# A transformer block on one core: some loads move to GpSimd's queue, weight splitting is spread, statistics go one by one, and three plain steps move ahead of a chunk's last down tiles

## The chip, the core and the metric

The kernel runs on one core of a Trainium2 chip. The metric is the device time in us of one execution. TensorE (PE) does the matrix products, VectorE (DVE), ScalarE (ACT) and GpSimd (POOL) the element work; each engine executes its own instructions in order. SyncE (SP), ScalarE and GpSimd issue DMA transfers; each has a queue of its own.

## What is computed

One block with adaptive layer norm: 32-head attention and a gated feed-forward layer over 2048 rows of width 512, all in 32-bit floats.

```python
B, S, D, F, H = 1, 2048, 512, 1792, 32
mod = (silu(c) @ w_mod)                      # six rows: sa, ca, ga, sb, cb, gb
h = layernorm(x) * (1 + ca) + sa
p = softmax((q @ k^T) * 16 ** -0.5)          # q, k, v from h @ wqkv, head size 16
x = x + ga * ((p @ v) @ wo)
h = layernorm(x) * (1 + cb) + sb
x = x + gb * ((silu(h @ w_gate) * (h @ w_up)) @ w_down)
```

## The kernel before, in words

**Precision.** Every operand of a large product is split into a high part and a low remainder, and three products (high by high, high by low, low by high) are summed. The splitting of `wo`, `w_gate`, `w_up` and `w_down` is done once, on GpSimd, by the generator `split_weights` (L573): it loads a raw piece, copies and subtracts, and stores the split tiles to `wo_dr`, `gu_dr` and `wd_dr` in DRAM. It has 24 pieces of work between its yields: the first loads, two for `wo`, then for each of seven pairs of gate and up tiles one piece for the gate half, one for the up half (in which both finished tiles of 1 MB are stored), and one for the down tile. `after` (L841) advances it by one piece at the end of every fourth step.

**Steps and units.** The order is written out by hand. Attention is cut into 32 units (8 groups of four heads by 4 chunks of 512 query rows) of 16 steps, 512 steps in all. A step has four pairs (`pair_of`, L877): a score product with its exponential on ScalarE (L504, L506), and a product for the row maxima of a unit 19 to 20 steps ahead, reduced on VectorE (L477, L479). Products with V follow (`pvs`). When the maxima of a unit are complete, VectorE combines them, TensorE transposes them, ScalarE copies them out, and SyncE writes them as two extra rows into the query tile (`max_rows`, L489 and L496, `qop<-mr`); the unit's scores read these rows. Keys and queries of the unit after next are loaded at a unit's sixth step (`load_k`, `load_q`, both through L402).

**Closing a unit.** `close_unit` (L823) sends the unit's sums through DRAM (`dn<-o`, `d_dr<-dn`, `rb<-d_dr`) on SyncE's queue, and five steps later GpSimd multiplies (L546) and stores to `o_dr` (L547). After a chunk's last unit, `begin` (L794) makes the chunk's tiles and issues the loads of its x rows (`load_x2`, L639) and of the two output weight tiles (`load_wo`, L644); one step later `load_o` (L659) brings the attention output back on GpSimd's queue, and `split_o` splits it on GpSimd.

**Plain and filled steps.** `plain` runs steps with nothing but attention; VectorE's reductions are then the main work beside TensorE's. `filled` runs two steps and mixes products of an earlier chunk into them: two output pairs (`out_pair`), then the jobs `gate_up` (24 by two products in halves) and `down`. Work on other engines that a finished job causes (the entries of `posts`) is issued by `hook` at the end of such a pair of steps. After an output pair, `add_o` (L726) adds the two row tiles to x and takes their statistics on VectorE. After the second pair, `scaled` (L802) computes the norm's scale (first steps on VectorE, the rest on GpSimd) and normalizes on GpSimd; then 9 plain steps, and 3 in which TensorE transposes the normalized rows (`turned`). A chunk starts at a fixed step (`STARTS`: 147, 275, 403), and the plain steps before the next chunk fill up to it.

**Middle tiles.** A gate tile ends with tanh on ScalarE, two operations on VectorE (L763, L765) and copy and subtract on GpSimd (L766, L767) into a middle tile (`tile_mid`, three buffers). `down` of pair m reads middle tiles 2m and 2m+1. For m below 6 a further gate tile stands between; tile 13 is directly followed by the last down.

**The end.** After step 512, seven jobs of chunk 2 are left (gate tiles 11, 12 and 13, downs of pairs 5 and 6, two halves each), and the whole of chunk 3 follows. The generator `rest` holds the seven jobs, three gate tiles first, then four downs; `take(rest, k)` issues k products between the steps of chunk 3's output projection (L748), of its statistics, `norm_scale` (on VectorE here), `normalize` (on ScalarE here, L687) and `turned`. A down tile has one buffer, so `load_wd` (L654) for pair 6 is issued when pair 5 is done. A spare query tile (`spare`) serves as the fourth middle tile.

Of the kernel before, what the change touches and what calls it, by code (L numbers as in the profile page):

```python
# [19 lines left out]
P = 128  # L20
# [81 lines left out]
def block_kernel(ctx, tc, x, wqkv, wo, w_gate, w_up, w_down, c, w_mod, out):  # L102
# [522 lines left out]
    class Chunk:  # L625
        def __init__(self, ci, x2, oT, hT):
            self.ci, self.x2, self.oT, self.hT = ci, x2, oT, hT
            self.w, self.wd, self.mid, self.mv, self.nt = {}, {}, {}, None, []
            self.places, self.ahead = None, 1
            self.jobs = [(gate_up, (0,)), (gate_up, (1,))]  # L630
            for m in range(NF // FG):
                if m:
                    self.jobs.append((gate_up, (2 * m + 1,)))
                if m + 1 < NF // FG:
                    self.jobs.append((gate_up, (2 * m + 2,)))
                self.jobs += [(down, (m, 0)), (down, (m, 2))]

        def load_x2(self):
            nc.sync.dma_start(self.x2, xd[:, 4 * self.ci:4 * self.ci + 4, :])  # L639

        def load_wo(self, places):
            self.wo = places
            for k, w in enumerate(places):
                nc.sync.dma_start(w.bitcast(F32), wo_dr[k])  # L644

        def load_gu(self, f):
            if f < NF:
# [78 lines left out]
    def add_o(ch, t0, outs):  # L726
# [7 lines left out]
        for e in range(2):  # L734
            t = t0 + e
# [3 lines left out]

    def out_pair(ch, t0, outs, halves):  # L740
        return accumulate(outs, lambda e, a, k: ch.oT[a][:, k, (t0 + e) * P:(t0 + e + 1) * P],
                          lambda b, k: ch.wo[k // 2][:, b, k % 2, :], NK,
                          lambda: posts.append(lambda: add_o(ch, t0, outs)), halves)
# [7 lines left out]
    def gate_up(ch, f, outs, halves):  # L751
# [3 lines left out]
        ch.mid[f] = mid = spare.pop(0) if spare and f == NF - 1 else tile_mid()  # L755
# [36 lines left out]
    side, spare = [], []  # L792

    def begin(ci):  # L794
# [4 lines left out]
        ch.load_x2()  # L799
# [43 lines left out]
    def after(i):  # L843
# [16 lines left out]
        if 0 <= i < UG and i % 4 == 3:  # L860
# [14 lines left out]
    def pair_of():  # L875
# [8 lines left out]
        done += 1  # L884

# [62 lines left out]
    for ci in range(last):  # L948
# [6 lines left out]
        scaled(ch)  # L955
# [4 lines left out]
        for _ in range(len(ch.jobs) - (KEEP if ci == last - 1 else 0)):  # L960
            job, args = ch.jobs.pop(0)
            work = job(ch, *args, outs, True)
# [3 lines left out]
            else:  # L966
                filled(SHORT, work)
    filled(none, iter(()), pairs=4)
# [21 lines left out]
    ch.load_x2()  # L990
    spare.append(pb.tile([P, 2, CW], F32R, name="qop", tag="qop", bufs=3))
    kept = chp.jobs
    rest = whole(chp, [j for j in kept if j[0] is gate_up] + [j for j in kept if j[0] is down])
# [5 lines left out]
    ch.load_o(nc.scalar, (NK - 1,))  # L999
    ch.split_o((NK - 1,), True)  # L1000
    take(rest, 36)
    for t in range(4):
        out_terms(ch, t, banks[t], (NK - 1,))
        if t % 2:
            add_o(ch, t - 1, banks[t - 1:t + 1])
    take(rest, 36)
    ch.norm_scale(nc.vector)
    ch.nt = [v_flat[:, (4 + 2 * k) * D:(6 + 2 * k) * D].rearrange("p (t d) -> p t d", t=2) for k in range(2)]
    for t in range(4):
        ch.normalize(t, True)  # L1010
    ch.places = [tile_gu() for _ in range(2)]
# [5 lines left out]
    take(rest, 24)  # L1017
# [28 lines left out]
```

## Time and profile before

| what | value |
|---|---|
| median of three runs | 1974.08 us (1966.42 to 1975.12) |
| profiled execution | 1970.09 us |
| its span, first to last instruction | 1968.3 us |
| mean granted clock of TensorE | 0.982 |
| busy, share of the span: PE / DVE / ACT / POOL | 96% / 80% / 63% / 21% |
| step 512 ends, last chunk alone from | about 1790.8 us to 1968.3 us |

In the profile, a row such as `PE bank L504 <- DMA qop<-mr` says that TensorE, at line 504 and about to write a bank, waited for the transfer from `mr` to `qop`. Tiles are called by the program's names: `qop` and `kop` are queries and keys, `x` the chunk's rows, `wgu` a gate and up tile (also used for `wo`), `wd` a down tile, `act` the chunk's attention output and later its normalized rows; near the end the last chunk lives in `kop` and `v_flat`. `SPq`, `POOLq` and `ACTq` are DMA issues and waits of those engines.

### The profile page before, as it was taken

What the parts mean: (1) busy time and instruction counts of PE and PEld (TensorE: products, weight loads), DVE (VectorE), ACT (ScalarE), POOL (GpSimd) and SP (SyncE); (2) the same over time, 40 slices, a digit from 0 to 9 for tenths busy, and PEclk for the clock granted to TensorE, in tenths of its full rate; (3) what the DMA queues carried; (4) which work ended last, traced back from release to release, by engine and by line L of the source; (5) the groups of instructions that cost most, each with busy time, mean ns of one, the idle gap of its engine ahead of it and who ended that gap; (6) DMA issues with size and microseconds to landing.
All of it is one profiled execution on the core that took longest, in us unless ns stands there. A gap on an engine that the chain in (4) does not pass through costs nothing.

```text
span 1968.3 us, 40520 instructions
## 1 busy us (share of the span) xinstructions
PE 1892.3 (96%) x16836; PEld 1170.6 (59%) x16836; DVE 1567.9 (80%) x2614; ACT 1240.7 (63%) x2284; POOL 408.2 (21%) x476
## 2 busy tenths in 40 slices
PE   6999999999989999999989999999989999998898
PEld 5766444444455666665455666666454566676687
DVE  5459998999979888887979888888979988822333
ACT  4222887788867666665867666666858866772100
POOL 2000465650013101111113101111112011130321
PEclk9999999999989999999999999999989999999999
DMA  8765676754444434443454334443532345332552
GB/s 283 268 221 130 185 215 204 226 182 85 99 111 100 105 116 120 134 116 85 101 117 97 99 115 131 117 117 95 122 90 53 96 107 147 122 111 103 214 193 107
DMA packets 80756, 267.59 MB, mean 136 GB/s; under 512 B 17364, under 2 KB 22484, under 8 KB 59892
## 3 DMA queue, kind: packets, MB, share of 16 engines
q1 hardware_dynamic: 67660, 212.81, 39.6%
q0 software_dynamic: 12224, 51.39, 7.7%
q8 instruction: 132, 2.16, 0.5%
q10 hardware_dynamic: 688, 0.80, 0.1%
q14 instruction: 52, 0.43, 0.1%
HBM read 201.85 MB, written 62.13 MB: 134 GB/s over the span
## 4 chain that ended last, share of the span: by engine, by line
PE 66%; DVE 24%; DMA 6%; ACT 2%; POOL 1%; issue 1%; SPq 0%; POOLq 0%; ACTq 0%; DVEq 0%
DVE mx L479 23%; PE bank L713 18%; PE bank L519 15%; PE bank L504 13%; PE bank L208 7%; PE bank L721 7%; PE bank L477 6%; DMA qop<-mr 2%; DMA rb<-d_dr 1%; DMA wgu<-gu_dr 1%; DMA qop<-qd 1%; PE bank L161 0%; PE bank L695 0%; DMA wm_ab<-in_w_mod 0%; DMA wd<-wd_dr 0%
## 5 line engine op out<-in xcount | busy, mean ns | idle before, releaser
L479 DVE TENSOR_REDUCE mx<-bank 128x1 f32<-128x512 f32 x2048 | 1302.8, 683 | 161.0 <-PE bank L477 121.3
L504 PE MATMUL bank<-qop,kop 50*128 50x512 f32 x2048 | 780.6, 436 | 32.4 <-DMA qop<-mr 20.6
L477 PE MATMUL bank<-kop,qop 48*128 48x512 f32 x2048 | 794.2, 441 | 6.4 <-DVE mx L479 3.9
L504 PEld LDWEIGHTS bank<-qop,kop 50*128 50x128 f32 x2048 | 360.6, 187 | 339.0 <-issue 82.4
L477 PEld LDWEIGHTS bank<-kop,qop 48*128 48x128 f32 x2048 | 356.5, 187 | 42.1 <-DVE mx L479 18.8
L713 PE MATMUL bank<-act,wgu 64*128 64x512 f32 x1872 | 305.0, 393 | 1.0 <-DVE mx L479 0.5
L713 PEld LDWEIGHTS bank<-act,wgu 64*128 64x128 f32 x1872 | 203.3, 187 | 33.4 <-DVE m L765 2.9
L713 PE MATMUL bank<-wd,mid 64*128 64x512 f32 x912 | 154.4, 399 | 3.0 <-POOL mid L766 2.2
L766 POOL CAST mid<-m 128x512 fp32r<-128x512 f32 x55 | 33.7, 613 | 593.5 <-PE bank L477 266.6
L546 POOL TENSOR_TENSOR on<-o,rb 128x512 f32<-128x512 f32 x31 | 39.7, 1282 | 546.8 <-DMA rb<-d_dr 332.7
L713 PEld LDWEIGHTS bank<-wd,mid 64*128 64x128 f32 x912 | 100.0, 189 | 21.3 <-POOL mid L766 3.0
L759 ACT ACTIVATE th<-bank 128x512 f32<-128x512 f32 x56 | 33.3, 597 | 111.2 <-PE bank L721 76.8
L208 PE MATMUL bank<-hT,wqs 128*128 128x512 f32 x384 | 97.0, 404 | 3.9 <-DVE prt L367 2.4
L763 DVE SCALAR_TENSOR_TENSOR q<-th,bank 128x512 f32<-128x512 f32 x56 | 38.1, 680 | 66.1 <-ACT th L759 66.1
L208 PEld LDWEIGHTS bank<-hT,wqs 128*128 128x128 f32 x384 | 71.5, 191 | 26.2 <-issue 5.9
L778 DVE TENSOR_TENSOR x<-bank,x 128x512 f32<-128x512 f32 x84 | 54.0, 682 | 34.9 <-PE bank L713 20.7
L767 POOL TENSOR_TENSOR mid<-m,mid 128x512 fp32r<-128x512 f32 x55 | 70.9, 1289 | 4.5
L367 DVE TENSOR_TENSOR prt<-bank,prt 128x512 fp32r<-128x512 f32 x32 | 21.9, 688 | 46.7 <-ACT prt L365 46.7
L721 PE MATMUL bank<-wd,mid 128*128 128x512 f32 x204 | 50.3, 398 | 7.8 <-DMA wd<-wd_dr 6.5
L365 ACT CAST prt<-bank 128x512 fp32r<-128x512 f32 x32 | 18.8, 587 | 59.6 <-PE bank L208 46.5
L765 DVE TENSOR_TENSOR m<-bank,q 128x512 f32<-128x512 f32 x56 | 38.7, 691 | 20.5 <-PE bank L721 18.4
L713 PE MATMUL bank<-wgu,act 64*128 64x512 f32 x288 | 48.5, 396 | 0.5 <-issue 0.5
(6274 smaller groups left out, 5112.2 us busy)
## 6 DMA issues: line engine op xcount, KB each, us to landing
wgu<-gu_dr SPq DMA_DIRECT2D x48, 1024.0 KB
kop<-kd SPq DMA_DIRECT2D x62, 768.0 KB
wd<-wd_dr SPq DMA_DIRECT2D x28, 1024.0 KB
gu_dr<-wgu POOLq DMA_DIRECT2D x14, 1024.0 KB, 5.1
qop<-qd SPq DMA_DIRECT2D x64, 192.0 KB
kd<-prt SPq DMA_DIRECT2D x16, 512.0 KB
qd<-prt SPq DMA_DIRECT2D x16, 512.0 KB
kop<-gu_dr SPq DMA_DIRECT2D x8, 1024.0 KB
```

What stands on the lines that cost most here:

```text
L208: nc.tensor.matmul(pt, lhs(a, k), rhs(b, k), start=(n == 0), stop=(n == 3 * nk - 1))
L477: nc.tensor.matmul(pm, qop[u][rows, s, qt * P:(qt + 1) * P], kop[u % 3][rows, s, kc * CW:(kc + 1) * CW], start=True, stop=True)
L479: nc.vector.tensor_reduce(mx[u][:, b, s, qt, kc:kc + 1], pm, op=ALU.max, axis=AX.X)
L504: nc.tensor.matmul(sp, kop[u % 3][rows, h // 2, kt * P:(kt + 1) * P], qop[u][rows, h // 2, :], start=True, stop=True)
L519: nc.tensor.matmul(pv[u][32 * h:32 * h + 32, cols], v_flat[:, e0:e0 + 32], p_[h][:, cols], start=(kt == 0 and half == 0), stop=(kt == 15), ...
L546: mul.tensor_mul(on, o, rb)
L713: nc.tensor.matmul(outs[e], lhs(e, a, k)[rows], rhs(b, k)[rows], start=(ph == 0 and j == 0), stop=(ph == 1 and j == z))
L721: nc.tensor.matmul(outs[e], lhs(e, a, k), rhs(b, k), start=(j == 0), stop=(j == z))
L763: nc.vector.scalar_tensor_tensor(q, th, 1.0, outs[0], op0=ALU.add, op1=ALU.mult)
L765: nc.vector.tensor_mul(m32, outs[1], q)
L767: nc.gpsimd.tensor_sub(mid[:, 1, :], m32, mid[:, 0, :].bitcast(F32))
L778: nc.vector.tensor_add(ch.x2[:, t, :], outs[e], ch.x2[:, t, :])
```

## The change

1. `load_wo` issues on GpSimd's queue instead of SyncE's, and `load_x2` takes the queue: GpSimd's for chunks 0 to 2, ScalarE's for chunk 3, there behind the load of the last part of o instead of ahead of all of it.
2. `split_weights` advances every fifth step (4, 9, ... 124) instead of every fourth (3, 7, ...).
3. Statistics of an output pair, and `scaled`, go into a list `side`, of which each pair takes one entry. At the end of the program `add_o` does them at once, as before.
4. In chunks 0 and 1, three plain steps stand between gate tile 13 and the last two downs. They come off the plain steps ahead of the next chunk.
5. The load of gate tile 12 of chunk 2 is issued in the last steps; a set `loaded` keeps it from being issued twice.
6. At the end the seven jobs keep their own order (tiles 11, 12, two downs, tile 13, two downs), the takes are 48, 24, 24 instead of 36, 36, 24, the loads of chunk 3's gate tiles come after the third, and the spare middle tile is gone.

```diff
-        def load_x2(self):
-            nc.sync.dma_start(self.x2, xd[:, 4 * self.ci:4 * self.ci + 4, :])
+        def load_x2(self, eng):
+            eng.dma_start(self.x2, xd[:, 4 * self.ci:4 * self.ci + 4, :])
...
-                nc.sync.dma_start(w.bitcast(F32), wo_dr[k])
+                nc.gpsimd.dma_start(w.bitcast(F32), wo_dr[k])
...
-            if f < NF:
+            if f < NF and f not in self.loaded:
+                self.loaded.add(f)
...
-        for e in range(2):
-            t = t0 + e
+
+        def sums(t):
             st = pf.tile([P, 6], F32, name="stt", tag="stt", bufs=2)
             nc.vector.bn_stats(st, ch.x2[:, t, :])
             nc.vector.bn_aggr(ch.mv[:, t, :], st)
 
+        for e in range(2):
+            if late:
+                side.append(lambda t=t0 + e: sums(t))
+            else:
+                sums(t0 + e)
...
-        ch.mid[f] = mid = spare.pop(0) if spare and f == NF - 1 else tile_mid()
+        ch.mid[f] = mid = tile_mid()
...
-        ch.load_x2()
+        ch.load_x2(nc.gpsimd)
...
-        if 0 <= i < UG and i % 4 == 3:
+        if 0 <= i < UG and i % 5 == 4:
             next(weights2, None)
...
         done += 1
+        if side:
+            side.pop(0)()
...
-        scaled(ch)
+        side.append(lambda: scaled(ch))
...
             job, args = ch.jobs.pop(0)
+            if args == (NF // FG - 1, 0):
+                plain(WIN)
...
+    chunks[last - 1].load_gu(NF - 2)
     filled(none, iter(()), pairs=4)
...
-    ch.load_x2()
-    spare.append(pb.tile([P, 2, CW], F32R, name="qop", tag="qop", bufs=3))
-    kept = chp.jobs
-    rest = whole(chp, [j for j in kept if j[0] is gate_up] + [j for j in kept if j[0] is down])
+    rest = whole(chp, chp.jobs)
...
     ch.load_o(nc.scalar, (NK - 1,))
+    ch.load_x2(nc.scalar)
     ch.split_o((NK - 1,), True)
-    take(rest, 36)
+    take(rest, 48)
...
-    take(rest, 36)
+    take(rest, 24)
...
+    take(rest, 24)
     ch.places = [tile_gu() for _ in range(2)]
...
     for f in range(ch.ahead):
         ch.load_gu(f)
-    take(rest, 24)
```

SyncE's instructions around the begin of chunk 0, before (`qop<-mr` in the first row belongs to the unit before, in the last row to the unit whose maxima are due at the begin):

```order
L496 DMA qop<-mr 2x8x128 x2
L530 DMA dn<-o 128x1x16
L535 DMA d_dr<-dn 128x16
L540 DMA rb<-d_dr 128x1x512
L402 DMA kop_959<-kd 48x2x2048 x2
L402 DMA qop<-qd 48x2x512 x2
L639 DMA x_5624<-in_A_x 128x4x512
L644 DMA wgu<-wo_dr 128x2048 x2
L496 DMA qop<-mr 2x8x128 x2
```

The same place in the changed kernel:

```order
L496 DMA qop<-mr 2x8x128 x2
L530 DMA dn<-o 128x1x16
L535 DMA d_dr<-dn 128x16
L540 DMA rb<-d_dr 128x1x512
L402 DMA kop_959<-kd 48x2x2048 x2
L402 DMA qop<-qd 48x2x512 x2
L496 DMA qop<-mr 2x8x128 x2
```

The x rows and the two output weight tiles no longer stand between the queries and the maxima. GpSimd's instructions at the same begin, before:

```order
L546 TENSOR_TENSOR on<-o,rb 128x512
L547 DMA o_dr<-on 128x512
L659 DMA act_5626<-o_dr 128x1x512 x4
L664 CAST act_5625<-act_5626 128x512
L665 TENSOR_TENSOR act_5626<-act_5626,act_5625 128x512
```

And in the changed kernel:

```order
L546 TENSOR_TENSOR on<-o,rb 128x512
L547 DMA o_dr<-on 128x512
L639 DMA x_5624<-in_A_x 128x4x512
L644 DMA wgu<-wo_dr 128x2048 x2
L660 DMA act_5626<-o_dr 128x1x512 x4
L665 CAST act_5625<-act_5626 128x512
L666 TENSOR_TENSOR act_5626<-act_5626,act_5625 128x512
```

They now stand between the store of the chunk's last attention output and its loads. ScalarE after the last attention step, before (`kop_86` and `v_flat` hold the last chunk, `th` is the tanh of tiles 11, 12 and 13, L687 normalizes, L700 scales a turned tile):

```order
L547 DMA o_dr<-on 128x512
L659 DMA kop_86<-o_dr 128x1x512
L664 CAST kop_86<-kop_86 128x512
L759 ACTIVATE th<-bank_69 128x512
L759 ACTIVATE th<-bank_67 128x512
L759 ACTIVATE th<-bank_69 128x512
L687 ACTIVATE v_flat<-v_flat,rs_20655,rs 128x512 x4
L700 ACTIVATE h_20793<-bank_63,modc 128x512
```

And in the changed kernel:

```order
L547 DMA o_dr<-on 128x512
L660 DMA kop_86<-o_dr 128x1x512
L639 DMA v_flat<-in_A_x 128x4x512
L665 CAST kop_86<-kop_86 128x512
L766 ACTIVATE th<-bank_69 128x512
L766 ACTIVATE th<-bank_67 128x512
L688 ACTIVATE v_flat<-v_flat,rs_20668,rs 128x512 x4
L766 ACTIVATE th<-bank_69 128x512
L701 ACTIVATE h_20789<-bank_63,modc 128x512
```

The load of x stands behind that of the last part of o, and the tanh of tile 13 stands behind the normalizing instead of ahead of it.

More of the change, by code (lines that the diff above doesn't have):

```diff
@@ L628, in __init__ @@
             self.w, self.wd, self.mid, self.mv, self.nt = {}, {}, {}, None, []
-            self.places, self.ahead = None, 1
+            self.places, self.ahead, self.loaded = None, 1, set()
             self.jobs = [(gate_up, (0,)), (gate_up, (1,))]
@@ L724, in accumulate, with add_o @@
                     yield
-    def add_o(ch, t0, outs):
+    def add_o(ch, t0, outs, late):
         if ch.mv is None:
@@ L742, in out_pair @@
                           lambda b, k: ch.wo[k // 2][:, b, k % 2, :], NK,
-                          lambda: posts.append(lambda: add_o(ch, t0, outs)), halves)
+                          lambda: posts.append(lambda: add_o(ch, t0, outs, True)), halves)
     def out_terms(ch, t, pt, ks):
@@ L791, in block_kernel @@
     chunks = {}
-    side, spare = [], []
+    side = []
     def begin(ci):
@@ L1004, in block_kernel @@
         if t % 2:
-            add_o(ch, t - 1, banks[t - 1:t + 1])
-    take(rest, 36)
+            add_o(ch, t - 1, banks[t - 1:t + 1], False)
+    take(rest, 24)
     ch.norm_scale(nc.vector)
```

## The prediction

> **What bounds the kernel now.** I read the page first, then TensorE's waits, then the places of the longest waits in the chain, in SyncE's issues and in the windows table.
>
> ```profile
> PE 1892.3 (96%) x16836; PEld 1170.6 (59%) x16836; DVE 1567.9 (80%) x2614; ACT 1240.7 (63%) x2284; POOL 408.2 (21%) x476
> DVE  5459998999979888887979888888979988822333
> ```
>
> TensorE is busy 96% of the span, so an edit can only remove what makes it stand still or run at half clock, or shorten the stretches where VectorE (the digits 9, the plain steps) sets the pace. TensorE's waits, in us in total, times and longest:
>
> ```profile
> PE bank L504 <- DMA qop<-mr: 20.6, 4, 6.4
> PE bank L721 <- DMA wd<-wd_dr: 6.5, 1, 6.5
> PE bank L748 <- ACT kop L664: 4.1, 1, 4.1
> PE bank L713 <- POOL mid L766: 2.2, 2, 2.0
> PE bank L477 <- DMA qop<-qd: 1.4, 1, 1.4
> PE bank L713 <- POOL mid L767: 0.8, 2, 0.4
> ```
>
> The change touches every one of them. The biggest is a small transfer: the two row maxima of a unit (8 KB each) that go into the query tile before its scores. SyncE's issues before the first of these waits, and the transfer's pieces in the chain (start, length):
>
> ```profile
> 522.47 0.90 SPq L402 DMA_DIRECT2D kop<-kd  x2
> 523.42 1.44 SPq L402 DMA_DIRECT2D qop<-qd  x2
> 524.90 0.46 SPq L639 DMA_DIRECT2D x<-in_A_x  x1
> 525.59 0.84 SPq L644 DMA_DIRECT2D wgu<-wo_dr  x2
> 545.23 1.34 SPq L496 DMA_DIRECT2D qop<-mr  x2
> ...
> 545.23 9.30 DMA qop<-mr
> 302.56 5.51 DMA qop<-mr
> ```
>
> At a chunk's begin the maxima stand in SyncE's queue behind about 5 MB: keys and queries (2 x 768 and 2 x 192 KB), x (1 MB) and the output weights (2 MB). They land 9.30 us after the first issue. The wait of 6.4 belongs to this place, so they are needed 9.30 - 6.4 = 2.9 us after issue.
>
> What such a wait costs is more than its length. Windows: start:end, width, busy us of PE, PEld, DVE, ACT, POOL, granted clock, DMA share, GB/s. The first is an undisturbed plain stretch, the next three are the chunk begins, the fifth is the wait at 302, the sixth the late queries.
>
> ```profile
> 505.00:525.00 20.00, 20.00 (x204) 9.49 (x202) 20.00 (x35) 17.14 (x34) 0.00 (x0) 1.00 0.09 22
> 545.00:565.00 20.00, 13.61 (x118) 6.08 (x118) 11.50 (x19) 10.19 (x20) 7.41 (x8) 0.74 0.38 97
> 985.00:1005.00 20.00, 14.02 (x127) 6.38 (x130) 12.39 (x21) 10.21 (x21) 7.40 (x8) 0.83 0.45 108
> 1420.00:1440.00 20.00, 14.30 (x121) 6.25 (x117) 12.36 (x22) 10.30 (x21) 7.72 (x9) 0.74 0.52 135
> 305.00:315.00 10.00, 7.40 (x50) 3.27 (x50) 5.45 (x10) 5.11 (x11) 8.59 (x9) 0.68 0.63 216
> 380.00:390.00 10.00, 8.56 (x69) 3.54 (x61) 8.59 (x16) 5.87 (x13) 9.15 (x10) 0.83 0.78 250
> ```
>
> VectorE sets the pace there, so its missing busy time is time lost: 20.00 - 11.50 = 8.5, 20.00 - 12.39 = 7.6, 20.00 - 12.36 = 7.6, together 23.7 us; at 302 it is 4.55, at 380 it is 1.4. The excess over the wait is the clock, granted at 0.68 to 0.83 in these windows.
>
> The Trainium skill ("TensorE: Matmul & The Clock Gate", Part 1) drops the clock only after an idle window of about 3.4 us. The row at 302 (a wait of 5.51 - 2.9 = 2.6 us) disagrees, since the clock fell after it. By the rule a remaining wait of 2.6 us would cost just that instead of 4.55, and the first term below would be about 4 us larger.
>
> **The change part by part.** *x and output weights to GpSimd's queue.* SyncE's maxima now have nothing large ahead but keys and queries, issued 22 us earlier. Yet the 3 MB still move then, out of another queue into the same engines. Is the maxima's time then the ordinary one, at most 2.9, or that of 302? There the other queue was full:
>
> ```profile
> q0 software_dynamic: 428, 2.60, 87.3%
> ```
>
> In 298 to 306 GpSimd's queue alone took 87.3% of the engines, and the maxima took 5.51. GpSimd issues at the first begin:
>
> ```profile
> 531.71 1.82 POOL L659 DMA_DIRECT2D act<-o_dr  x3
> 556.70 1.27 POOL L665 TENSOR_TENSOR act<-act,act 128x512 fp32r<-128x512 f32 x1
> L713 PE MATMUL bank<-wgu,act x96: 385/392/498, 565.3 to 590.6; 64*128 64x512 f32 x96
> ```
>
> x and weights will be issued at 531.7, just ahead of these loads of o. With 3 MB and four times 256 KB, 4 MB, at 250 GB/s (estimated between the 216 and the 325 that 2.60 MB in 8 us make) the queue is full until about 548, so the maxima at 545 meet it. Bounds of the remaining loss per begin: 0 and 4.55; below zero is excluded, since the maxima cannot land before they are needed with profit. I take 3.6, nearer to 302, whose queue was as full. Gain: 23.7 - 3 x 3.6 = 12.9 us, bounds 10.0 and 23.7.
>
> The same FIFO puts the loads of o behind 3 MB. Today the last split of o ends at 556.7 + 1.3 = 558.0, and its first use is at 565.3. All the bytes are the same and the engines were full until about 552 anyway, so o comes at most a few us later, in order of use, while the chunk starts some 5 us earlier: cost 0, hidden by these 7 us; without that cover it would be 2 to 4 us per begin.
>
> *Weight splitting every fifth step.* Work per splitting step is unchanged, its cover is the plain steps. The two-store steps of a pair of tiles stood one step before the maxima at 302 (step 43 and maxima at 44); now they stand at 24, 39, 54, and so on, never within three steps before maxima. This removes 4.55, and perhaps the 1.4 at 380:
>
> ```profile
> 368.33 14.40 DMA qop<-qd
> ```
>
> But loads of keys and queries come at steps 21, 37, 53, 69, 85, 101, 117, and the two-store steps at 24, 39, 54, 69, 84, 99, 114: every load now meets one. Queries took 14.40 there with a wait of 1.4, so 13.0 us are free. I charge three new losses of the 1.4 kind, 4 us. Net gain 4.55 + 1.4 - 4 = 2, bounds -6 and +6.
>
> *Statistics one by one.* After the second output pair VectorE runs two adds, two statistics and the scale's first steps in a row, and TensorE starves. Windows again; the first is ordinary chunk work, the second a chunk's end, the third the statistics.
>
> ```profile
> 900.00:920.00 20.00, 19.64 (x204) 12.87 (x204) 17.11 (x27) 13.02 (x23) 1.29 (x1) 1.00 0.62 145
> 920.00:930.00 10.00, 7.72 (x42) 4.64 (x46) 5.04 (x9) 3.47 (x6) 2.49 (x3) 0.66 0.26 68
> 1035.00:1045.00 10.00, 8.70 (x65) 3.51 (x61) 9.32 (x21) 6.12 (x13) 6.53 (x22) 0.83 0.00 0
> ```
>
> VectorE sets the pace after it, so 10.00 - 9.32 = 0.7 is lost, three times: gain 2, bounds 0 and 4 (TensorE's own gap of 1.3, three times). Norm scaling starts three pairs later, under nine plain steps.
>
> *Three plain steps ahead of the last down tiles.* The last down needs the middle tile of the gate tile right before it. At 920 TensorE waits 2.0 + 0.4 and the clock falls: VectorE does 5.04 where ordinary work does 17.11 / 2 = 8.56, so 3.5 / 8.56 of 10 us are lost, 4.1 us. The other of the two times is the rest of 2.2 + 0.8, that is 0.6 us. The moved steps are taken from the stretch before the next chunk, at one price. Gain 4.7, bounds 0 and 4.7.
>
> *The end.* TensorE's rows after the last attention, then the end of the norm scale on VectorE, the normalizing on ScalarE, and two groups of the page:
>
> ```profile
> 1799.04 8.42 PE L721 MATMUL bank<-act,wgu 128*128 128x512 f32 x36
> 1811.60 5.49 PE L748 MATMUL bank<-kop,kop 128*128 128x512 f32 x12 [4.13 <-ACT kop L664]
> 1825.30 5.66 PE L721 MATMUL bank<-wd,mid 128*128 128x512 f32 x24
> 1837.86 1.62 PE L721 MATMUL bank<-wd,mid 128*128 128x512 f32 x3 [6.46 <-DMA wd<-wd_dr]
> 1846.33 2.47 PE L721 MATMUL bank<-kop,wgu 128*128 128x512 f32 x10
> ...
> 1826.31 0.17 DVE L683 TENSOR_SCALAR rs<-rs 128x4 f32<-128x4 f32 x1
> 1826.51 2.94 ACT L687 ACTIVATE v_flat<-v_flat,rs,rs 128x512 f32<-128x512 f32 x4 [3.12 <-DVE rs L683]
> L778 DVE TENSOR_TENSOR x<-bank,x 128x512 f32<-128x512 f32 x84 | 54.0, 682 | 34.9 <-PE bank L713 20.7
> L767 POOL TENSOR_TENSOR mid<-m,mid 128x512 fp32r<-128x512 f32 x55 | 70.9, 1289 | 4.5
> ```
>
> 48 products at 8.42 / 36 = 0.234 last from 1799.0 to 1810.3, so the wait for the last part of o shrinks from 4.13 to about 1.3 and its 12 products run in 2.8 at full clock: done at 1814.4. The next wd tile is asked for after the earlier downs, one gate tile (5.6 us) before its use: the 6.46 goes. What is late next is the normalizing: VectorE's chain from 1811.6 to 1826.5 gets two adds of 0.682 more, and ScalarE ends at 1826.5 + 1.4 + 2.9 = 1830.8. TensorE reaches the transposes at about 1829.4, because the second down's bank is read behind the statistics. Then the last middle tile, whose tanh stands behind the normalizing on ScalarE and whose copies stand behind those of the first turned tile on GpSimd, takes about 3.4 us (two pairs of copies, each 1.3 and about 0.6). The remaining products and transposes took 1846.33 - 1837.86 = 8.5. So the last chunk starts at 1830.8 + 3.4 + 8.5 = 1842.7, against 1846.3: gain 3.6, and 0.5 from a shorter load chain with x no longer beside it: 4. Bounds: 0 (x, now behind the last o on ScalarE's queue, 2 us late, and half clock) and 8.
>
> Sum: 12.9 + 2 + 2 + 4.7 + 4 = 25.6. The profiled execution took 1970.09 with a span of 1968.3; 1970.1 - 25.6 = 1944.5. It lies 4 under the median of the runs and 4 above the fastest; the four executions average 1.3 above it, so I forecast 1945.
>
> **The rivals.** *The queue was everything* (0.2): maxima from an otherwise empty queue land in 2.9 us. For it: 28 of 32 units show no wait, some with weight traffic. Against it: 302. All 23.7 come back, the splitting gains 6: 23.7 + 6 + 2 + 4.7 + 4 = 40.4, 1930. The Trainium skill ("DMA: Bandwidth & Descriptors", Queues, rings and completion order) says that each DMA engine goes round between its queues packet by packet; that speaks for this one.
>
> *The engines were everything* (0.2): the maxima land as late as before whatever their queue, and 12.9 falls to 0 to 3. For it: 302, and the full engines. The sum is 13 to 16, 1955, and 1964 if the end gives nothing either. The same page (Issuing engines are not separate DMA queues) says that all issuers' transfers interleave on the same 16 engines and only issue time is saved.
>
> *Slower* (0.06): the splitting's new rhythm. If each of the seven loads of keys and queries lands 6 us later than the 13.0 that are free, each costs what a chunk begin costs now, about 8: 56 lost instead of 4, 1944.5 + 52 = 1997. It decides from 5 us per load on, where 25.6 is eaten up. Against it: the looser rhythm moves fewer bytes in any 13 us than now.
>
> **How the numbers follow.** My forecast, 1937 to 1953, has 0.54. Between it and the rivals the cases run from 1928 to 1963, with 1 in 10 left out on either side. About 0.5%, 10 us, is what a measurement can tell from no change: faster means under 1964. The forecast and the first rival are (0.74), and 0.08 of the second, whose rest is within: 0.82 faster, 0.12 within, 0.06 slower.
>
> **What would show it.** Right: the waits for maxima at the three begins fall from about 6 to 1 to 3 us, with windows there at 16 or more of 20; no wait for wd near the end; the middle tile's wait gone in the chunks; the last chunk's first gate tile starts some 26 us earlier. Wrong: waits of 5 us or more for maxima at the begins, waits for keys or queries in the splitting steps, a wait for the output weights or o at a chunk's start, or a TensorE gap over 5 us before the last chunk's transposes.

## The result and the profile after

Four executions of the changed kernel took 1949.57 us in the median (1946.00 to 1950.91), four of the kernel before beside them 1974.17 (1966.42 to 1975.12). The ratio is 0.9881, with a 95% interval of 0.9853 to 0.9909. The profiled execution took 1946.00 with a span of 1944.2, against 1970.09 and 1968.3: 24.1 us of span are gone, and the mean granted clock is 0.992 against 0.982.

From the page: the engines' busy times hardly differ from before, so what went is standing still and half clock.

```profile
PE 1884.0 (97%) x16836; PEld 1166.5 (60%) x16836; DVE 1568.0 (81%) x2614; ACT 1241.2 (64%) x2284; POOL 415.6 (21%) x487
```

**Where the time went.** Each unit's maxima are sent off by one pair of issues on SyncE (L496), in both kernels at the same place of the program. They serve as milestones. Issue times, and the lengths of the stretches between them:

| stretch, by units | before | after | gain |
|---|---|---|---|
| start to 1 | to 182.72 | to 181.78 | 0.94 |
| 1 to 9 (weight splitting) | to 504.38: 321.66 | to 502.03: 320.25 | 1.41 |
| 9 to 10 | to 545.23: 40.85 | to 542.87: 40.84 | 0.01 |
| 10 to 11 (begin of chunk 0) | to 604.33: 59.10 | to 597.03: 54.16 | 4.94 |
| 11 to 16 | to 885.03: 280.70 | to 877.68: 280.65 | 0.05 |
| 16 to 18 (last downs of chunk 0) | to 986.99: 101.96 | to 974.30: 96.62 | 5.34 |
| 18 to 19 (begin of chunk 1) | to 1045.21: 58.22 | to 1029.96: 55.66 | 2.56 |
| 19 to 24 | to 1325.85: 280.64 | to 1310.59: 280.63 | 0.01 |
| 24 to 26 (last downs of chunk 1) | to 1423.36: 97.51 | to 1407.17: 96.58 | 0.93 |
| 26 to 28 (begin of chunk 2) | to 1524.33: 100.97 | to 1503.44: 96.27 | 4.70 |
| 28 to 32 | to 1733.31: 208.98 | to 1712.48: 209.04 | -0.06 |
| 32 to the end | to 1968.3: 234.99 | to 1944.2: 231.72 | 3.27 |

The gain falls where the change put its edits: 12.2 at the three begins (queue and statistics together), 6.3 at the two chunk ends, 3.3 at the end. The 1.4 in the splitting is no measured gain: six profiled executions that have the same code there take 318.5 to 323.7 us, and the kernel before took 318.10 when it was profiled again. The first row's 0.9 lies ahead of every edit; executions differ there by up to about 3 us, which is why stretches and not only spans are compared below.

TensorE's waits of the changed kernel (us in total, times, longest):

```profile
PE bank L504 <- DMA qop<-mr: 11.2, 4, 3.9
PE bank L722 <- DVE q L770: 5.0, 1, 5.0
PE bank L722 <- POOL mid L773: 3.5, 2, 2.7
...
PE bank L477 <- DMA kop<-kd: 0.8, 1, 0.8
PE bank L477 <- DMA qop<-qd: 0.8, 1, 0.8
```

The wait for wd (6.5) and that for the last part of o (4.1) are gone; the maxima are still waited for, four times. SyncE's issues at chunk 0's begin, and the transfers in the chain:

```profile
520.09 0.90 SPq L402 DMA_DIRECT2D kop<-kd  x2
521.04 1.30 SPq L402 DMA_DIRECT2D qop<-qd  x2
542.87 1.34 SPq L496 DMA_DIRECT2D qop<-mr  x2
...
303.38 5.20 DMA qop<-mr
443.13 16.26 DMA qop<-qd
542.87 6.25 DMA qop<-mr
974.30 6.83 DMA qop<-mr
1407.17 5.54 DMA qop<-mr
```

SyncE has issued nothing else for 20 us, yet these 16 KB take 6.25 us, where 2.9 would do. At the three begins they take 6.25, 6.83 and 5.54 (before 9.30, 8.88, 8.51) and are waited for 3.3, 3.9 and 2.6. GpSimd's rows at that place say what is in the way (start, length, in brackets the idle time before and what ended it):

```profile
529.35 0.77 POOL L639 DMA_DIRECT2D x<-in_A_x  x1
530.10 1.08 POOL L644 DMA_DIRECT2D wgu<-wo_dr  x2
...
547.83 0.61 POOL L665 CAST act<-act 128x512 fp32r<-128x512 f32 x1 [9.87 <-DMA act<-o_dr]
554.24 1.28 POOL L666 TENSOR_TENSOR act<-act,act 128x512 fp32r<-128x512 f32 x1
```

x and the output weights go out at 529.35 and 530.10, and o, in the same queue behind them, is there only by 547.83, so the queue is at work when the maxima are issued at 542.87. Windows of the changed kernel: the three begins, the end of chunk 0, the statistics of chunk 1 (start:end, width, busy us of PE, PEld, DVE, ACT, POOL, granted clock, DMA share, GB/s):

```profile
541.00:561.00 20.00, 16.51 (x150) 8.20 (x152) 14.75 (x24) 12.05 (x24) 7.37 (x8) 0.83 0.32 80
972.00:992.00 20.00, 15.72 (x138) 6.72 (x136) 13.78 (x23) 11.39 (x23) 7.37 (x8) 0.83 0.37 88
1405.00:1425.00 20.00, 17.07 (x162) 9.07 (x162) 16.05 (x27) 13.37 (x26) 7.39 (x8) 0.91 0.28 70
...
915.00:935.00 20.00, 19.30 (x193) 11.74 (x191) 17.89 (x31) 13.42 (x25) 2.19 (x4) 1.00 0.16 56
...
1019.00:1030.00 11.00, 10.35 (x101) 4.55 (x92) 10.54 (x25) 6.80 (x14) 3.46 (x18) 1.00 0.10 41
```

At the begins VectorE misses 5.2, 6.2 and 3.9 of 20 us, 15.4 together, where it missed 23.7 before. At the chunk's end and in the statistics the clock is full again (before 0.66 and 0.83).

The end, TensorE's rows:

```profile
1778.31 11.17 PE L722 MATMUL bank<-act,wgu 128*128 128x512 f32 x48
1789.31 2.93 PE L755 MATMUL bank<-kop,kop 128*128 128x512 f32 x12
...
1799.96 4.60 PE L722 MATMUL bank<-wd,mid 128*128 128x512 f32 x12 [4.95 <-DVE q L770]
...
1813.94 2.14 PE L722 MATMUL bank<-wd,mid 128*128 128x512 f32 x3 [2.74 <-POOL mid L773]
1822.03 2.46 PE L722 MATMUL bank<-kop,wgu 128*128 128x512 f32 x10
```

The 12 products with the last part of o follow the 48 without a wait, and no wait for wd is left. A wait of 4.95 stands in their place, for VectorE's part of gate tile 12, which is queued there behind the adds and statistics; and these are late because x is:

```profile
1782.76 0.86 ACTq L639 DMA_DIRECT2D v_flat<-in_A_x  x1
1793.64 1.29 DVE L734 TENSOR_TENSOR v_flat<-bank,v_flat 128x512 f32<-128x512 f32 x2 [4.83 <-PE bank L722]
DMA to landing us min/median/max: 10.1/10.2/10.5
```

The last row is that of all loads of x. The last chunk's is issued at 1782.76 and so lands at about 1793.0, 0.6 before the adds; the products for the first add ended about 2 us before that. (The row of the adds names a TensorE bank; releasers are inferred. In three of the experiments below, which have the same code here, VectorE's idle time ahead of these adds, 2.0 to 2.9 us, is put down to `DMA v_flat<-in_A_x`.) From the first product of the output projection to the last chunk's first gate tile it is 1822.03 - 1770.01 = 52.0 us, against 1846.33 - 1790.75 = 55.6 before (the starts are TensorE's first L755 and L748 rows).

### The profile page after: what moved, and what is told of

Its sections match the earlier page's. It is cut to its first block, busy times and chain, and to the rows that moved or that the text cites. A ratio compares the mean times of both kernels' runs of the same rounds, so it can differ in the third digit from the quotient of the medians.

```text
span 1944.2 us, 40515 instructions
## 1 busy us (share of the span) xinstructions
PE 1884.0 (97%) x16836; PEld 1166.5 (60%) x16836; DVE 1568.0 (81%) x2614; ACT 1241.2 (64%) x2284; POOL 415.6 (21%) x487
## 4 chain that ended last, share of the span: by engine, by line
PE 69%; DVE 25%; DMA 3%; ACT 2%; POOL 0%; issue 0%; SPq 0%; POOLq 0%; ACTq 0%
DVE mx L479 23%; PE bank L714 18%; PE bank L519 16%; PE bank L504 13%; PE bank L722 7%; PE bank L477 7%; PE bank L208 6%; DMA qop<-mr 1%; DMA qop<-qd 1%; PE bank L755 1%; DVE stt L738 1%; PE bank L696 0%; PE bank L161 0%; DMA wm_ab<-in_w_mod 0%; PE bank L277 0%
## 5 line engine op out<-in xcount | busy, mean ns | idle before, releaser
L722 PE MATMUL bank<-wd,mid 128*128 128x512 f32 x216 | 55.9, 410 | 9.2 <-DVE q L770 5.0
L722 PEld LDWEIGHTS bank<-wd,mid 128*128 128x128 f32 x216 | 41.7, 196 | 20.4 <-DVE q L770 5.4
```

The source lines that it names most:

```text
L722: nc.tensor.matmul(outs[e], lhs(e, a, k), rhs(b, k), start=(j == 0), stop=(j == z))
```

## The experiments

The theory: the maxima's time depends on the order in their queue and also on what other queues move at that moment, so the change shortened the begins without clearing them. The rivals: that only the bytes in flight count (then the queue's change bought nothing), and that the begins were never about the queue. Further ones concern the other parts. "After" is the changed kernel; each experiment changes it by the lines shown. Gains are read between the milestones of the table, in one profiled execution of each kernel; where several kernels have the same code at a place, their range says how much a single difference is worth. Kernels that were run several times beside the kernel before have a ratio to it; the others were run once.

### The queue alone undone

```diff
-                nc.gpsimd.dma_start(w.bitcast(F32), wo_dr[k])
+                nc.sync.dma_start(w.bitcast(F32), wo_dr[k])
...
-        ch.load_x2(nc.gpsimd)
+        ch.load_x2(nc.sync)
```

> The changed kernel with the x rows of chunks 0 to 2 and all output weight tiles back on SyncE's queue; the rest of the change stays. Theory (queue order counts): the waits for the row maxima at the three begins go back from 3.3, 3.9 and 2.6 us to about 6 each, and the span grows by 8 to 10 us (the loss at the begins is 23.7 us in the kernel before and 15.4 us in the changed one), to about 1953. Rival (only the bytes in the 16 engines count, whatever the queue): the waits stay near 3 us and the span within 2 us of 1944.

Measured: 1959.56 us, ratio 0.9938 (0.9920 to 0.9956), span 1950.9. TensorE's wait and the transfers in the chain of this kernel:

```profile
PE bank L504 <- DMA qop<-mr: 17.1, 3, 6.7
```

```profile
542.02 9.60 DMA qop<-mr
977.90 8.32 DMA qop<-mr
1411.83 7.88 DMA qop<-mr
```

The old landing times are back. From unit 10 to 11, 18 to 19 and 26 to 27 it takes 58.67, 56.83 and 56.44 us; after takes 54.16, 55.66 and 52.79. So the queue alone is worth 4.5 + 1.2 + 3.6 = 9.3 us against the changed kernel's profile, and 6.9 to 8.7 against four further executions with the same begins as the changed kernel. The whole time agrees: the interval of the ratio lies above that of the changed kernel (0.9853 to 0.9909), and the profiled execution, 1952.73, was the fastest of ten. The rival that only bytes count has fallen. The begin of chunk 1 gains least: there the clock falls as far with the short wait (0.83 in the window) as with the long one before (0.83).

### The loads of x and weights some 20 us earlier

```diff
-                at(i + 6, lambda: begin(u // NG))
+    for c in range(last):
+        at(16 * NG * (c + 1), lambda c=c: begin(c))
```

Nothing is left out; begin(c) now comes at steps 128, 256 and 384, ahead of the store of the chunk's last attention output.

> The changed kernel with the begin of chunks 0 to 2 (loads of x rows and output weights) at steps 128, 256 and 384, some eight steps earlier, so that these 3 MB have mostly moved before the row maxima are due. Theory (what is left of the waits is the full DMA engines): the waits for the maxima at the begins fall from 3.3, 3.9 and 2.6 us to under 1 and the span falls by 10 to 15 us, to 1929 to 1934. Rival (what is left is the path of this transfer itself, or GpSimd's queue): the waits stay at 3 us, span 1942 to 1946. A second rival: the early loads press on the keys and queries issued then; waits for queries appear, of 1 to 3 us, and half of the gain is lost.

Measured: 1947.24 us, ratio 0.9872 (0.9839 to 0.9904), span 1944.6: no faster than after. At chunks 1 and 2 no maxima are waited for any more, which shows that the 3 MB were what they met. At chunk 0, GpSimd is ahead of its steps and issues x at 501.18; so the bytes met the maxima of the unit before, issued at 505.66, which took 7.06 and were waited for 2.9. Even at chunk 1, where the wait has gone, not all of its time came back. From the wait list of 935 to 990, from VectorE's rows, and a window:

```profile
PE bank L477 <- DVE mx L479: 0.8, 1, 0.8
```

```profile
976.07 0.71 DVE L485 TENSOR_SCALAR nm<-m 128x16 fp32r<-128x16 f32 x1
976.81 0.52 DVE L486 SCALAR_TENSOR_TENSOR nm<-m,nm 128x16 fp32r<-128x16 f32 x1
```

```profile
980.00:985.00 5.00, 5.00 (x37) 1.79 (x29) 2.81 (x5) 1.83 (x4) 2.39 (x3) 0.50 0.01 3
```

A single wait of 0.8 us, and the clock was granted at 0.50 for the next 5 us. The little operations that combine the maxima took 0.71 and 0.52 us while GpSimd was splitting o beside them; in the kernel before, where GpSimd is idle at that point, they take 0.18 and 0.17. The stretch from unit 17 to 19 is 3.4 us shorter than before (after: 0.95), 25 to 27 is 5.35 shorter (after: 3.85), and 9 to 11 only 2.7 (after: 4.95). The cause of the waits is thus shown; that their whole cost comes back with them is not.

### Early begin with chunk 0 on SyncE's queue, and the splitting of o later

```diff
-                at(i + 6, lambda: begin(u // NG))
+    for c, i in enumerate((126, 256, 384)):
+        at(i, lambda c=c: begin(c))
...
-                nc.gpsimd.dma_start(w.bitcast(F32), wo_dr[k])
+                (nc.gpsimd if self.ci else nc.sync).dma_start(w.bitcast(F32), wo_dr[k])
...
-        ch.load_x2(nc.gpsimd)
+        ch.load_x2(nc.gpsimd if ci else nc.sync)
```

Besides, `split_o` is called at step i + 11 instead of i + 9. SyncE issues in time with the steps, so chunk 0's bytes go out right behind one unit's maxima (x at 507.11, the maxima at 505.73 and 547.79).

> The changed kernel with the loads of x rows and output weights early and apart from other work: for chunk 0 on SyncE's queue right behind the maxima of step 124, for chunks 1 and 2 on GpSimd's at steps 256 and 384; and the splitting of o two steps later, behind the two small VectorE steps that make the maxima. Theory (the full engines held the maxima, and beside GpSimd's splitting VectorE's small steps run three times as long and the clock falls): no wait for maxima over 1 us at any begin, clock 1.0 there, and 10 to 14 us less from the maxima before a begin to those after it, three begins together; span 1930 to 1935. Rival (the loss moves on: the later splitting is late for the output products): TensorE waits for the split o at a chunk's start, 1 to 3 us each, and the span stays above 1938.

Measured: 1939.76 us, ratio 0.9865 (0.9835 to 0.9894), span 1936.1. The interval overlaps that of the changed kernel, so the stretches have to tell the two apart. The begins:

```profile
545.00:565.00 20.00, 19.52 (x176) 10.33 (x176) 18.00 (x31) 14.32 (x28) 4.35 (x5) 0.91 0.01 2
972.00:992.00 20.00, 19.20 (x185) 10.46 (x187) 19.41 (x35) 16.29 (x32) 6.36 (x7) 1.00 0.04 14
1400.00:1420.00 20.00, 18.73 (x179) 10.10 (x176) 19.48 (x33) 15.66 (x30) 6.11 (x7) 1.00 0.03 9
```

VectorE is busy 18.00 to 19.48 of 20 us at all three; no maxima are waited for there. Against before, 9 to 11, 17 to 19 and 25 to 27 gain 7.5, 7.2 and 6.7 us, 11.6 more than after does. So the 15.4 us that the changed kernel still loses at its begins were for the most part the loads'. The other half of the edit did nothing: GpSimd splits o when o lands, whatever the step, and at 972.60 and 972.94 the little operations ran beside it as in the run above, and took 0.30 and 0.52. That the clock held here and not there is not explained by the later call. The last experiment below has the same code at that place and gained 4.9 and 7.0 us from 17 to 19 and from 25 to 27, with a clock of 0.91 and 1.00 in these two windows. Of the eight begins of this kind in the three early-begin kernels, the clock fell (to 0.50 to 0.79 in a window of 5 us) after waits for VectorE of 0.7, 0.8, 1.1 and 1.1 us, and held at 1.00 after 0.5, 0.6, 0.9 and 0.9. What decides it is open.

### The three plain steps taken out

```diff
-            if args == (NF // FG - 1, 0):
-                plain(WIN)
```

> The changed kernel without the three plain steps ahead of the last down tiles of chunks 0 and 1. Theory (the last middle tile is late there, since GpSimd stands waiting for the reciprocals): the wait of 2 us and the half clock after it come back in chunk 0, and the span grows by 5 to 6 us (5.3 and 0.9 by the times of the maxima), to about 1950. Rival (the plain steps only shift the phase of the queues): the wait for the middle tile stays under 0.5 us and the span changes by under 2 us.

Measured: 1951.53 us, ratio 0.9900 (0.9868 to 0.9932), span 1949.8; the interval overlaps that of the changed kernel. From 16 to 18 it takes 97.30 us and from 24 to 26 97.56; after takes 96.62 and 96.58. The plain steps are worth 0.7 + 1.0 = 1.7 us here, not the 6.3 of the table. The rest belongs to something else, which the next run was to find.

### The kernel before, once more

Unchanged.

> The kernel before, unchanged, profiled a second time. Theory (the long wait at the end of chunk 0, about 2.4 us with the half clock after it, came from a store on GpSimd that stood 1.73 us before it was issued, which some executions have and some don't): if the gap is again 1.7 us, the wait for the middle tile is 2 us or more; if it is 0.3 us, the wait is under 0.8 and this stretch is 4 to 5 us shorter. Rival (the wait belongs to the kernel): 2 us or more whatever the gap. The waits for the maxima at the begins are again 5.5 to 6.5 us under either.

Measured: 1966.06 us, span 1964.3. GpSimd's store at the end of chunk 0, in the run without plain steps and then here:

```profile
917.56 0.58 POOL L547 DMA_DIRECT2D o_dr<-on  x1 [0.30 <-POOL on L546]
```

```profile
916.64 0.60 POOL L547 DMA_DIRECT2D o_dr<-on  x1 [1.73 <-DVE mx L479]
```

```profile
920.00:930.00 10.00, 9.35 (x80) 6.05 (x78) 7.68 (x12) 5.76 (x10) 1.10 (x2) 0.83 0.17 62
```

The issue of the store comes 1.73 us after the multiplication instead of 0.30. In the kernel before the middle tile's copy is queued right behind it on GpSimd, and TensorE, which needs that tile for the last down, waits 1.7 + 0.4 here (2.0 + 0.4 in the first profile) and then runs at 0.83 of the clock. 16 to 18 takes 100.40 us. With plain steps, the same delay of 1.73 was there in the kernel with the queue undone, and 16 to 18 took 96.61, as after did without the delay. So the three plain steps are worth 0.7 us where the store is issued at once, and 100.40 - 96.61 = 3.8 to 101.96 - 96.61 = 5.3 where it is delayed.

The delay goes with the kernel, not with the execution. In each of the twelve traces of this document exactly one DMA issue of GpSimd stands about 1.7 us behind its data with no wait that accounts for it (the releaser named above is inferred). In five traces it is this store: the kernel before twice, the queue undone, the second early begin and the last experiment, in all of which chunk 0's x and output weights go out on SyncE's queue. In the seven in which they go out on GpSimd's it is an earlier store, at 627 to 633; in the changed kernel:

```profile
626.73 0.65 POOL L547 DMA_DIRECT2D o_dr<-on  x1 [1.69 <-issue]
```

Ahead of the late issue GpSimd has issued 64 transfers in each of the five and 62 in each of the seven. At its earlier place it costs nothing: 11 to 16 takes 280.65 us in the changed kernel, 280.70 before. So the queue's edit, by putting three more transfers into GpSimd's queue, also moves the late issue away from the chunk's end. That is where most of the gain from 16 to 18 came from: without the plain steps it is already 101.96 - 97.30 = 4.7 us of the 5.3. Why one issue is late at all is open.

### Statistics at once

```diff
-            add_o(ch, t0, outs, True)
+            add_o(ch, t0, outs, False)
...
-        side.append(lambda: scaled(ch))
+        scaled(ch)
```

> The changed kernel with the statistics of an output pair and the norm's scale issued at once, as before. Theory (TensorE starves behind the burst and the clock falls): a TensorE gap of about 1 us and a granted clock of 0.8 to 0.9 come back after the second output pair of each chunk, and the stretch from a chunk's begin to the next maxima is 1 to 1.5 us longer, 3 to 4 us in all. Rival (VectorE has the same work either way): under 1 us in all.

Measured: span 1948.0. From the second add to the next maxima's issue it takes 10.50, 11.85 and 11.85 us at the three chunks; after takes 10.44, 10.43 and 10.46, before 11.86, 11.85 and 11.85. The window at chunk 1 of this kernel, beside after's at 1019:

```profile
1020.00:1032.00 12.00, 10.69 (x95) 4.65 (x87) 11.18 (x24) 6.44 (x13) 6.46 (x22) 0.86 0.09 36
```

With all at once the clock falls to 0.86, one by one it stays at 1.00. That is 1.4 us a chunk; at chunk 2 the next unit gives 0.8 of it back (42.70 here, 43.49 after). Against the kernel before, the statistics are worth 3 x 1.4 - 0.8 = 3.4 us. Against this run it is 2.1, since at chunk 0 the burst did no harm here, and against the second profile of the kernel before 2.8, where it did none at chunk 2 (10.46). One by one, all 27 stretches of nine profiles lie between 10.40 and 10.81.

### Splitting every fourth step

```diff
-        if 0 <= i < UG and i % 5 == 4:
+        if 0 <= i < UG and i % 4 == 3:
```

> The changed kernel with the weight splitting advanced every fourth step again. Theory (the two rhythms cost about the same, each losing at other places): from the first maxima to those of unit 9 the time is within 2 us of the changed kernel's 320.3 us, where the kernel before took 321.7. Rival (the spread splitting is a gain of its own): 3 us or more longer.

Measured: span 1946.7. From unit 1 to 9 it takes 319.57 us, after takes 320.25 and before 321.66, all within the 318.5 to 323.7 of equal code. The old rhythm inside the new kernel is no slower: the spread splitting has no gain that these runs can tell from none. Where it loses, it loses as the others do: maxima of 5.15 us at 303.12, queries of 15.27 at 366.52.

### The last chunk's x first

```diff
+    ch.load_x2(nc.sync)
     rest = whole(chp, chp.jobs)
...
-    ch.load_x2(nc.scalar)
```

> The changed kernel with the last chunk's x rows loaded as before, on SyncE's queue ahead of the last load chain; the rest stays. Theory (x arrives late behind the last part of o: issued at 1782.8, needed by about 1790.8, used at 1793.6): the additions of the output projection start 2 to 3 us earlier, TensorE's wait of 5.0 us in the downs shrinks to 2 to 3, and the span falls by 2 to 3 us, to about 1942. Rival (x beside the load chain of o delays that chain by as much): the last part of o is split 1 to 2 us later, and the span stays within 1 us of 1944.

Measured: 1949.90 us, ratio 0.9891 (0.9859 to 0.9923), span 1947.1. The wait for tile 12 falls from 5.0 to 2.2 us, and a new one of 1.5 for the last part of o takes its place. From the output projection to the first gate tile it is 1824.93 - 1773.45 = 51.5, against 52.0, and 50.4 to 52.4 in the seven profiles with the changed kernel's end (in which the wait for tile 12 is 2.8 to 5.0): x ahead of the short chain of loads delays that chain by nearly as much as it saves. Moving a megabyte ahead of another need only chooses which of the two is late.

### The old order of the last jobs

The seven jobs as in the kernel before (three gate tiles, then four downs, takes of 36, 36 and 24, the spare middle tile), with x still behind o on ScalarE's queue.

```diff
-    rest = whole(chp, chp.jobs)
+    spare.append(pb.tile([P, 2, CW], F32R, name="qop", tag="qop", bufs=3))
+    kept = chp.jobs
+    rest = whole(chp, [j for j in kept if j[0] is gate_up] + [j for j in kept if j[0] is down])
...
-    take(rest, 48)
+    take(rest, 36)
```

> The changed kernel with the old order of the seven jobs at the end (three gate tiles first, takes of 36, 36 and 24, the spare middle tile back), but x still behind the last part of o on ScalarE's queue. Theory (the new order removes the wait for the down tile and shortens the one for o, and gives part back at the statistics): from the output projection's first product to the last chunk's first gate tile it takes 55 to 56 us as in the kernel before, against 52.0, and the wait for wd of 6 us is back. Rival (the gain came from x no longer beside the load chain): 52 to 53 us.

Measured: span 1951.4, and 1829.28 - 1774.87 = 54.4 us for the stretch. TensorE's rows:

```profile
1792.65 3.29 PE L755 MATMUL bank<-kop,kop 128*128 128x512 f32 x12 [1.06 <-ACT kop L665]
...
1819.84 1.62 PE L722 MATMUL bank<-wd,mid 128*128 128x512 f32 x3 [4.44 <-DMA wd<-wd_dr]
```

The wait for wd is back with 4.44. So of the 3.6 us that the end gained, 2.4 are the order of the jobs and 1.2 the place of x; against the mean of the seven profiles with the changed kernel's end, 51.3, the order gives 3.1. With the same 36 products ahead of it as in the kernel before, the last part of o is waited for 1.06 us instead of 4.13: with x out of its chain of loads it is there 3.1 us earlier. A wait of 3.39 for tile 12, behind the late x, takes most of that back.

### The early begins, and x of the last chunk four steps before the end

The kernel of early begin with chunk 0 on SyncE's queue, and:

```diff
-    ch.load_x2(nc.scalar)
+    at(n - 4, lambda: chunks[last].load_x2(nc.gpsimd))
...
+    take(rest, 25)
...
-    take(rest, 24)
```

The third take now stands ahead of the normalizing loop, so that tile 13's tanh comes before it on ScalarE.

> The kernel with the early loads at the begins and the later splitting of o, and at the end two more edits: the last chunk's x rows are loaded on GpSimd's queue four steps before the last step, ahead of the load chain, and gate tile 13 is issued ahead of the normalizing, with one product of the last downs, so that its tanh and its middle tile come before those of the turned rows. Theory (x late, then the middle tile late, is what is left at the end): the wait of 5.0 us in the downs falls to 1 to 3, that of 2.7 for the middle tile under 0.5, the stretch from the output projection to the last chunk's first gate tile falls from 52.0 to 46 to 49, span 1930 to 1934. Rival (VectorE's chain sets this stretch): waits move to the transposes, and the stretch stays above 50.

Measured: 1932.60 us (1925.74 to 1937.08), ratio 0.9798 (0.9762 to 0.9834), span 1930.7: the fastest version, 0.8% below the changed kernel by the ratios, whose intervals don't touch. TensorE's rows:

```profile
1783.78 2.93 PE L755 MATMUL bank<-kop,kop 128*128 128x512 f32 x12
...
1791.09 3.04 PE L722 MATMUL bank<-wd,mid 128*128 128x512 f32 x12 [1.60 <-DVE q L770]
...
1808.41 2.46 PE L722 MATMUL bank<-kop,wgu 128*128 128x512 f32 x10
```

The stretch takes 1808.41 - 1764.49 = 43.9 us against 52.0, and the wait for tile 12 falls from 4.95 to 1.60. The wait for tile 13's middle tile falls from 2.74 to 0.40. Here x is early without standing ahead of o, and 8.1 us come back, so the late x and the late tile 13 together were what bounded the changed kernel's end; this run doesn't separate them.

## Why the prediction was right, point by point

**The sum.** 25.6 us were forecast against the profiled execution, 24.1 were found, and nearly all of the gain lies in the forecast stretches. That the sum came so close is in part luck: the maxima fell about 4 us short of their term, the chunk ends gave 1.6 more than theirs for a reason that the prediction didn't have, and 0.9 lies ahead of every edit. Three steps failed: the price of the remaining loss at the begins, the cause of the wait at chunk 0's end, and the place of the next wait at the end. Two numbers don't follow from their working: two pairs of copies of 1.3 and 0.6 make 3.8 us and not 3.4, and the second rival without the end comes to 1961 and not 1964.

**Maxima and queue: 12.9 forecast, about 8.5 measured.** The mechanism held: SyncE's queue no longer delays the maxima, the bytes in GpSimd's queue still do, as the row at 302 had shown. From the maxima's issue to the second pair of output adds it is 8.7 us shorter in the three begins together (47.24, 46.37, 46.40 before; 43.72, 45.23, 42.32 after). The six profiles with the loads on GpSimd's queue at the old steps take 131.3 to 133.7 us for these three together, the three with the loads on SyncE's 140.0 to 142.9: 8.5 between the means. The step that failed is the price of a remaining loss: 3.6 per begin, at most 4.55, "the queue was as full" as at 302. Measured were 5.2, 6.2 and 3.9. At 302 the maxima land in 5.51; at the first two begins they took 6.25 and 6.83. The queue was not as full as at 302 but fuller: from 539 to 547 GpSimd's queue took 96.0% of the engines in the changed kernel, against 87.3%. One row was taken as the upper end where it was a sample.

Of the two rules set beside it, the round between queues packet by packet (the Trainium skill, "DMA: Bandwidth & Descriptors", Queues, rings and completion order) would, as the prediction used it, have brought a few KB in a queue of their own through in the ordinary 2.9 us, which 6.25 us does not show. The other (the same page, Issuing engines are not separate DMA queues), that only issue time is saved, is contradicted too: the landing fell from 9.60 to 6.25 by the queue alone. The begins' gain of 8.5 lies between what the two rivals make of it (23.7, and 0 to 3), nearer to the second.

**o cost nothing.** This held. The last split of o ended at 554.24 + 1.28 = 555.5 against 558.0, and no wait for it stands in TensorE's list.

**Splitting: 2 forecast, no gain measured.** The 1.4 of the table lies inside the scatter of equal code, and the working failed. "Never within three steps before maxima" fails at once: the maxima of step 44 waited again, with 5.20 us and 1.3 of wait. GpSimd's rows before it:

```profile
286.64 1.28 POOL L546 TENSOR_TENSOR on<-o,rb 128x512 f32<-128x512 f32 x1 [19.23 <-DMA rb<-d_dr]
...
302.29 0.58 POOL L585 DMA_DIRECT2D wd_dr<-wd  x1 [0.30 <-POOL wd L582]
```

GpSimd stood 19.23 us for the unit's sums, and then did the pieces of several steps in a row. A table of step numbers says when a piece is issued in program order; it is no time. That the loads of keys and queries meet the stores was right (16.26 us at 443, two waits of 0.8); the slower rival needed 8 us for each of seven loads. With the rhythm of four in the new kernel the stretch is as long, so the edit was worth nothing that can be measured, and its forecast of 2 held only by its bounds of 6 either way.

**Statistics: 2 forecast, 2.1 to 3.4 measured.** Right: the clock stays at 1.00 where it was 0.83.

**Chunk ends: 4.7 forecast, 6.3 measured, the size by luck.** The place, the waiting tile and the clock were right, and the plain steps do protect the tile (96.61 with the store late). The step that failed is the cause of the wait, and with it which edit removes it. What the prediction took for the ordinary dependence of the last down on its middle tile was mostly a store issue on GpSimd that came 1.73 us after its data instead of 0.30. In the changed kernel the queue's edit has already moved that delay elsewhere, so that of the 6.3 the plain steps give 0.7 + 1.0. The trace of before held the number, in the row of the store ahead of the copies, and the prediction did not read what the copies were queued behind.

**The end: 4 forecast, 3.3 to 3.6 measured, 4.4 between the means (55.7 in two profiles before, 51.3 in seven after).** The wait for o, expected to shrink to 1.3, went, since o came 3.1 us earlier with x out of its chain, and that for wd went. The step that failed is what is late next. It was not the normalizing ahead of the transposes: TensorE shows no wait there in the changed kernel. It waited 4.95 earlier, in the downs, for tile 12's part on VectorE, because x landed about 10 us after its issue, behind o, and the adds ahead of that part waited for it. The bound "x 2 us late" was there and should have been the value. The last middle tile, forecast to take 3.4, was waited for 2.74. The order of the jobs gave 2.4 to 3.1 of the forecast 3.6, x's new place 1.2 where 0.5 was forecast.

**Clock.** The prediction set the row at 302 against the rule that the clock falls only after an idle window of about 3.4 us (the Trainium skill, "TensorE: Matmul & The Clock Gate", Part 1). The runs bear the row out: waits of 3.3, 3.9 and 2.6 us, 9.8 together, cost 15.4 us of VectorE's work, with 0.83 to 0.91 granted. Only the 3.9 is longer than the rule asks; and once a wait of 0.8 us was followed by 5 us at 0.50.

## What to carry to other kernels

A queue of its own takes a small urgent transfer out of the line but not out of the traffic: send large loads so that they finish before the next urgent transfer is due, and check which transfer they meet instead. Where an engine is not tied to the steps of the program (GpSimd here), a later or earlier place in the code need not move the work in time; an engine that is tied to them (SyncE) does move it. Price a wait from more than one row, and of a gap read also what the late instruction was queued behind on its own engine. Two edits that remove the same wait share one gain: take each out alone before it is credited.

## What was not expected of the hardware

- Two transfers of 8 KB, alone in SyncE's queue, took 5.54 to 6.83 us to land while GpSimd's queue moved 3 MB and o; at the 28 units where TensorE does not wait they land before they are needed, which at the begins is 2.9 us after their issue.
- The granted clock fell after short waits: to 0.50 for 5 us after one of 0.8. After others of 0.9 it held at 1.00.
- Two small VectorE operations took 0.71 and 0.52 us beside GpSimd's splitting, where they take 0.18 and 0.17 with GpSimd idle.
- In every trace one DMA issue of GpSimd came 1.69 to 1.73 us after its data and the stores around it 0.30 us after. In the kernel before it was the same store in both traces; with three more transfers in GpSimd's queue it was an earlier one, in all seven traces. What causes it is open.
